# Pooled-key attention and channel mix on one core: the left-over keys of both heads of a pair in one matmul on a tile of 32 rows by 128 columns, in front of the burst

## The chip, the core and the metric

The kernel runs on one core of one Trainium2 chip. The metric is device time in microseconds (us), the median of several runs; lower is better.

## What is computed

Attention over pooled keys, then a channel mix (a gated feed-forward layer) on the attention's output. Batch 8, 8 heads, 576 tokens, head dimension 64; keys and values are averaged over groups of 8 tokens, so that 72 keys are left for each head.

```python
k_p = k.reshape(B, H, Sp, pool, D).mean(axis=3)
v_p = v.reshape(B, H, Sp, pool, D).mean(axis=3)
scores = scale * np.matmul(q, k_p.transpose(0, 1, 3, 2))
scores = scores - np.max(scores, axis=-1, keepdims=True)
attn = np.exp(scores)
attn = attn / (np.sum(attn, axis=-1, keepdims=True) + 1e-09)
attn_out = np.matmul(attn, v_p)              # the second product
# x: the heads side by side, 512 channels
xk = mu_k * x + (1.0 - mu_k) * x_prev        # x_prev: x one token earlier
xr = mu_r * x + (1.0 - mu_r) * x_prev
k = np.maximum(xk @ w_k, 0.0)
v = k * k @ w_v
r = 1.0 / (1.0 + np.exp(-(xr @ w_r)))
return r * v
```

## The kernel before, in words

The 4,608 tokens are cut into 13 chunks: one of 128, one of 256 and eleven of 384 tokens. For each chunk the scores, the softmax, the second product, the token shift and the three matrix products of the channel mix (`hidden`, line 1182, `gate`, line 1231, `mixed`, line 1264) are issued. A small list scheduler (class `Order`) decides at build time in which order the steps of all chunks stand on each engine; each step tells it the engine and a length, and it takes due times from a table (`EARLIER`). The order is fixed in the built program. TensorE does nearly all of the time's work: the channel mix alone runs as triples of matmuls on a high and a low part of each operand.

The change is in `quarters`, which makes the second product of one of the eleven chunks of 384 tokens (chunks 2 to 12). The 72 keys of a head are split into 64 main keys and 8 left-over keys. The probabilities come out of VectorE's transposes 32 rows by 32 columns at a time: `pth` (line 926) holds those of the main keys, `ptq` (line 955) those of the left-over keys. Each of the four 32-row groups of the array (index `t`) takes one quarter of the chunk's tokens, 96 columns, and writes its own PSUM bank of the four-bank tile `quad`. For each pair of heads `g` (4), three products `j` are added up: two blocks of 32 main keys (`j` 0 and 1, weights `vq_main`) and the left-over keys (`j` 2, weights `vq_rest`). In a 32-row group the left-over rows are 4 heads by 8 keys; `vq_rest` has a copy of the values for every head with zeros in the rows of the other heads, and so picks its head. For each of the two heads `m` of a pair the product goes to its own half of the array's columns. So a chunk has 4 x 3 x 4 x 2 = 96 matmuls, each on a tile of 32 rows by 64 columns, all at line 1033 and all on end: a burst. A matmul on fp32 data runs as two passes, each a weight load (PEld in the profile) and a matmul (PE), so that a burst has 192 of each.

What stands around a burst on TensorE are matmuls on the whole array of 128 by 128: those of `gate` or `hidden` in front of it, those of `mixed` or `gate` behind it. The scores of three tokens' tiles (line 795) form a similar burst, on tiles of 64 rows by 64 columns. Behind a burst ScalarE reads `quad` (`t`, line 1085), VectorE reads it (`xm`, line 1127), and ScalarE and GpSimd split the result into `xkh`, `xkl`, `xrh` and `xrl` for the next chunk. From chunk 7 on `hidden` places an alignment instruction (line 1174) on TensorE's queue, which fills up to 64 slots with NOPs, or branches over more, so that the next burst begins at a fixed place in a block of 256 instructions.

Of the kernel before, what the change touches and what calls it, by code (L numbers as in the profile page):

```python
# [17 lines left out]
B, H, S, D = 8, 8, 576, 64  # L18
# [4 lines left out]
NPAIR = H // 2  # L23
# [237 lines left out]
def attention_then_channel_mix(  # L261
# [13 lines left out]
    nc = tc.nc  # L275
# [28 lines left out]
    vq_main = [const.tile([P, 4, NPAIR, D], F32, name=f"vq_main{i}") for i in range(2)]  # L304
    vq_rest = [const.tile([P, 2, 4, D], F32, name=f"vq_rest{i}") for i in range(2)]
# [11 lines left out]
    def operand(kind, c):  # L317
        if c in WHOLE:
            return whole_operands[kind]
        if (kind, c) not in operands:  # L320
            whole = {"pth": range(len(CHUNKS)), "xkh": WHOLE_HID, "xrh": WHOLE_GATE, "sh": WHOLE_MIX, "ptq": range(len(CHUNKS))}.get(kind, ())
            dtype = F32 if c in whole else F32R
            operands[kind, c] = sb.tile(shapes[kind], dtype, name=f"{kind}_{c}", tag=kind)
        return operands[kind, c]
# [40 lines left out]
    for tag, n in EARLY:  # L365
        t = sb.tile([P, n, 2 * POOL * KEYS], F32, name=f"early_{tag}", tag=tag)
# [638 lines left out]
    def ready(c):  # L1005
        mine = [i for i, t in enumerate(tiles) if t[0] == c]
        return (
            *[(k, i) for i in mine for k in ("main", "side")], "om",
            *([("rest", 0)] if c in WHOLE_ATT else [("late rest", b) for b, *_ in units[c]]),
            *[("values", b, p) for b, *_ in units[c] for p in range(2)], *([] if c in WHOLE_ATT else [("turned", b) for b, *_ in units[c]]),  # L1010
        )

    def quarters(c):

        yield need(*ready(c))
        sc = yield take("sc")
        hi = yield take("hi")
        yield "pe", 2.75, False
        main = operand("pth", c).rearrange("p g n -> p (g n)").rearrange("p (i j k) -> p i j k", j=16, k=32)
        rest = operand("ptq", c)  # L1020
        quad = joint["quad"]
        out = quad[:, :, :CH].rearrange("p t (g i k) -> p t g i k", g=NPAIR, k=32)
        batch = [next(b for b, _, n, at in units[c] if at <= CH // 4 * t < at + n) % 2 for t in range(4)]
        for g in range(NPAIR):
            for j in range(3):
                for t, i in enumerate(batch):
                    rows = slice(32 * t, 32 * t + 32)
                    for m in range(2):
                        if j < 2:
                            w, p = vq_main[i][rows, (t - 2 * m - j) % 4, g], main[rows, :, 4 * g + 2 * m + j, :]  # L1030
                        else:
                            w, p = vq_rest[i][rows, g // 2, 2 * (g % 2) + m], rest[rows, :, g // 2, :]
                        nc.tensor.matmul(  # L1033
                            out=out[m * D:(m + 1) * D, t, g], lhsT=w, rhs=p, start=(j == 0), stop=(j == 2),
                        )
        for g in range(NPAIR):
            held["out", c, g] = quad[:, :, g * CH // 4:(g + 1) * CH // 4]
            order.make(("attended", c, g))
        held["quad", c] = [sc, hi, NPAIR]
# [274 lines left out]
    for c, n in enumerate(CHUNKS):  # L1314
        if c not in WHOLE_ATT:
            order.add(att_due[c], quarters(c), SPARE)
        for g in range(NPAIR):
            order.add(att_due[c] + g, attended(c, g), SPARE if c > 1 else 0.0)
            if c in WHOLE:
                order.add(att_due[c] + g + 6, later_joined(c, g))  # L1320
        for jt in range(NJT):
            order.add(begin[c] + 0.0455 * n * jt / NJT, hidden(c, jt), 1.0 if c else 0.0)
        for tt in range(n // P):
            order.add(begin[c] + 0.0455 * n + 2.8 * tt, gate(c, tt))
            order.add(begin[c] + (0.0455 + 0.022) * n + 5.5 * tt, mixed(c, tt))
# [56 lines left out]
```

## Time and profile before

| what | value |
|---|---|
| runs (3) | 597.18, 598.83 and 599.61 us; median 598.83 |
| profiled execution, span from first to last instruction | 595.8 us |
| median of the runs less that span | 3.0 us |
| TensorE matmuls busy | 588.2 us, 99% of the span |
| weight loads busy | 508.3 us, 85% |
| VectorE, ScalarE, GpSimd busy | 58%, 49%, 38% |
| line 1033's share of the chain that ended last | 4% |
| granted TensorE clock | 1.000 (2.4 GHz), mean over the span |

The page gives the profiled execution's span alone; its own time is not listed apart from the three runs. The chain that ended last is followed back from the last instruction; from 146.6 us on it consists of TensorE's pieces alone, up to the last 4 us.

### The profile page before, as it was taken

To read this page: it belongs to the slowest core of one execution; us is meant where nothing else is said; L and a number is where in the kernel's file an instruction comes from. 1 tells how busy PE (TensorE), PEld (TensorE's weight loads), DVE (VectorE), ACT (ScalarE), POOL (GpSimd) and SP (SyncE) were. 2 spreads that over 40 slices of the span, in tenths; PEclk is the share of its full clock that TensorE was granted. 3 is DMA by queue.
4 is the path that set the end of the run, shared out by engine and by line. 5 is a ranking of instruction groups with operands and counts; after the bars stand their busy time and mean duration, and the time that the engine had idled before them with its cause. 6 is when DMAs were issued, how large, how long until landed. Compare 5 with 4: busy or idle time off the path is not lost.

```text
span 595.8 us, 14121 instructions
## 1 busy us (share of the span) xinstructions
PE 588.2 (99%) x5822; PEld 508.3 (85%) x5822; DVE 348.5 (58%) x709; ACT 294.3 (49%) x574; POOL 224.9 (38%) x350
## 2 busy tenths in 40 slices
PE   9999999999999999999999999999999999999997
PEld 8986458888989989988988988988988988988985
DVE  4989956876438725944814944664824833834411
ACT  4777665844462453553642552462652643554420
POOL 2520269458051552346232257148114115115000
PEclk9999999999999999999999999999999999999999
DMA  8697422442005214113003221521201101000001
GB/s 308 212 390 287 157 77 89 137 157 72 2 19 204 73 46 165 73 57 96 20 12 120 95 73 57 192 73 56 78 2 62 47 1 40 15 3 36 19 0 53
DMA packets 23055, 54.72 MB, mean 92 GB/s; under 512 B 2896, under 2 KB 6352, under 8 KB 22992
## 3 DMA queue, kind: packets, MB, share of 16 engines
q1 hardware_dynamic: 22992, 53.82, 25.8%
q8 instruction: 46, 0.75, 0.5%
q14 instruction: 17, 0.14, 0.1%
HBM read 41.23 MB, written 9.44 MB: 85 GB/s over the span
## 4 chain that ended last, share of the span: by engine, by line
PE 84%; DVE 5%; POOL 4%; DMA 3%; ACT 2%; issue 1%; SPq 1%; DVEq 0%; POOLq 0%; ACTq 0%
PE mm L1264 26%; PE mm L1182 24%; PE mm L1231 11%; PE bank L1182 6%; PE quad L1033 4%; PE bank L1231 4%; PE bank L1264 4%; PE quad L795 3%; DMA got_wr<-in_w_r 2%; POOL stage L577 1%; POOL xkl L1153 1%; POOL xrl L1153 1%; PE own L441 1%; DVE xm L1127 1%; DVE stage L577 1%
## 5 line engine op out<-in xcount | busy, mean ns | idle before, releaser
L1182 PE MATMUL mm<-xkh,w_k 128*128 128x384 f32 x576 | 147.5, 336 | 1.2 <-DVE rk L1199 0.9
L1264 PE MATMUL mm<-w_v,sh 128*128 128x512 f32 x464 | 146.8, 392 | 0.0
L1127 DVE SCALAR_TENSOR_TENSOR xm<-quad,given,t 128x384 f32<-128x384 f32 x88 | 50.3, 613 | 109.2 <-ACT t L1085 72.5
L1182 PEld LDWEIGHTS mm<-xkh,w_k 128*128 128x128 f32 x576 | 103.6, 188 | 3.2 <-DVE rk L1199 1.7
L1264 PEld LDWEIGHTS mm<-w_v,sh 128*128 128x128 f32 x464 | 87.1, 188 | 19.0
L1182 PE MATMUL mm<-xkl,w_k 128*128 128x384 f32 x288 | 96.5, 335 | 0.5 <-POOL xkl L1153 0.5
L1264 PE MATMUL mm<-w_v,sl 128*128 128x512 f32 x232 | 90.4, 390 | 0.0
L1205 ACT CAST sh<-rk 128x384 fp32r<-128x384 f32 x88 | 45.1, 512 | 58.8 <-DVE rk L1199 58.6
L881 POOL TENSOR_TENSOR px<-e,sm 128x64 f32<-128x64 f32 (+1 forms) x33 | 13.7, 414 | 157.3 <-DVE sm L871 79.9
L1231 PE MATMUL mm<-w_r,xrh 128*128 128x512 f32 x192 | 61.3, 391 | 0.0
L1207 DVE TENSOR_TENSOR sl<-rk,sh 128x384 fp32r<-128x384 f32 x88 | 53.4, 608 | 12.8 <-ACT sh L1205 12.7
L1274 DVE TENSOR_TENSOR rs<-mm,rs 128x512 f32<-128x512 f32 x32 | 22.0, 688 | 64.9 <-PE mm L1264 64.5
L1153 POOL TENSOR_TENSOR xkl<-xm,xkh 128x384 fp32r<-128x384 f32 x44 | 44.3, 1019 | 41.3 <-ACT xkh L1151 41.3
L1182 PEld LDWEIGHTS mm<-xkl,w_k 128*128 128x128 f32 x288 | 54.1, 188 | 1.1 <-POOL xkl L1153 1.1
L1192 ACT ACTIVATE rk<-mm 128x384 f32<-128x384 f32 x72 | 35.0, 487 | 39.4 <-PE mm L1182 38.4
L1085 ACT ACTIVATE t<-quad,om_sb 128x384 f32<-128x384 f32 x88 | 44.9, 580 | 17.7 <-PE quad L1033 17.7
L1264 PEld LDWEIGHTS mm<-w_v,sl 128*128 128x128 f32 x232 | 43.6, 188 | 8.8
L577 POOL TENSOR_TENSOR stage<-stage 128x512 f32<-128x512 f32 (+4 forms) x56 | 48.1, 862 | 7.5 <-DMA stage<-in_vm 4.9
L1153 POOL TENSOR_TENSOR xrl<-xm,xrh 128x384 fp32r<-128x384 f32 x44 | 44.3, 1017 | 3.0 <-ACT xrh L1151 3.0
L1199 DVE SCALAR_TENSOR_TENSOR rk<-mm,rk 128x384 f32<-128x384 f32 x72 | 39.6, 550 | 8.3 <-ACT rk L1192 7.2
L1231 PEld LDWEIGHTS mm<-w_r,xrh 128*128 128x128 f32 x192 | 36.0, 188 | 7.7
L1231 PE MATMUL mm<-w_r,xrl 128*128 128x512 f32 x96 | 37.5, 390 | 0.0
(159 smaller groups left out, 978.6 us busy)
## 6 DMA issues: line engine op xcount, KB each, us to landing
qs<-in_qT SPq DMA_DIRECT2D x36, 256.0 KB, 4.1
out<-rs SPq DMA_DIRECT2D x36, 256.0 KB, 2.0
stage<-in_kT SPq DMA_DIRECT2D x15, 576.0 KB, 5.4
stage<-in_vm SPq DMA_DIRECT2D x15, 512.0 KB, 6.2
got_wk<-in_w_k SPq DMA_DIRECT2D x8, 512.0 KB, 6.8
got_wv<-in_w_v SPq DMA_DIRECT2D x8, 512.0 KB, 10.4
stage<-in_vr SPq DMA_DIRECT2D x6, 512.0 KB, 3.5
got_wr<-in_w_r SPq DMA_DIRECT2D x4, 512.0 KB, 8.6
```

The lines of the kernel that those rows point to most:

```text
L577: nc_eng.tensor_tensor(out=st[:, :, :w], in0=st[:, :, :w], in1=st[:, :, w:2 * w], op=ALU.add)
L1033: nc.tensor.matmul(out=out[m * D:(m + 1) * D, t, g], lhsT=w, rhs=p, start=(j == 0), stop=(j == 2),)
L1085: nc.scalar.activation(out=by_token(ts[m][:, 1:n + 1]), in_=xp, func=AF.Copy, scale=om_sb[:, m, g:g + 1])
L1127: nc.vector.scalar_tensor_tensor(out=by_token(xm[:, :n]), in0=bank[:, :n] if c in WHOLE_ATT else bank, scalar=mu_sb[:, m, g:g + 1], in1=by ...
L1153: nc.gpsimd.tensor_tensor(out=lo, in0=xm[:, :n], in1=hi, op=ALU.subtract)
L1182: nc.tensor.matmul(out=hp, lhsT=w[:, o], rhs=x[:, ct, :n], start=(ct == 0 and k == 0), stop=(ct == NCT - 1 and k == len(terms) - 1),)
L1192: nc.scalar.activation(out=rk[:, :n], in_=hp, func=AF.Relu)
L1199: nc.vector.scalar_tensor_tensor(out=rk[:, :n], in0=hp, scalar=0.0, in1=rk[:, :n], op0=ALU.max, op1=ALU.mult)
L1205: nc.scalar.copy(out=sh[:, :n], in_=rk[:, :n])
L1207: nc.vector.tensor_tensor(out=operand("sl", c)[:, jt, :n], in0=rk[:, :n], in1=sh[:, :n], op=ALU.subtract)
L1231: nc.tensor.matmul(out=bank, lhsT=x[:, ct, o], rhs=w, start=(ct == 0 and k == 0), stop=(ct == NCT - 1 and k == len(terms) - 1),)
L1264: nc.tensor.matmul(out=bank, lhsT=s[:, o], rhs=w, start=(jt == 0 and k == 0), stop=(jt == NJT - 1 and k == len(terms) - 1),)
```

## The change

The left-over keys are taken out of the inner loop. They come first, for all four pairs, and the two heads of a pair share one matmul: its weights are two neighbouring blocks of `vq_rest`, 128 columns, its output all 128 partitions, its tile 32 rows by 128 columns. The first of them in each bank opens the sums of the whole bank, and the last of the 64 main matmuls closes them. A burst has 16 + 64 = 80 matmuls, or 160 passes.

```diff
         for g in range(NPAIR):
-            for j in range(3):
+            for t, i in enumerate(batch):
+                rows = slice(32 * t, 32 * t + 32)
+                nc.tensor.matmul(
+                    out=out[:, t, g],
+                    lhsT=vq_rest[i][rows, g // 2, 2 * (g % 2):2 * (g % 2) + 2].rearrange("p m d -> p (m d)"),
+                    rhs=rest[rows, :, g // 2, :], start=(g == 0), stop=False,
+                )
+        for g in range(NPAIR):
+            for j in range(2):
                 for t, i in enumerate(batch):
                     rows = slice(32 * t, 32 * t + 32)
                     for m in range(2):
-                        if j < 2:
-                            w, p = vq_main[i][rows, (t - 2 * m - j) % 4, g], main[rows, :, 4 * g + 2 * m + j, :]
-                        else:
-                            w, p = vq_rest[i][rows, g // 2, 2 * (g % 2) + m], rest[rows, :, g // 2, :]
                         nc.tensor.matmul(
-                            out=out[m * D:(m + 1) * D, t, g], lhsT=w, rhs=p, start=(j == 0), stop=(j == 2),
+                            out=out[m * D:(m + 1) * D, t, g], lhsT=vq_main[i][rows, (t - 2 * m - j) % 4, g],
+                            rhs=main[rows, :, 4 * g + 2 * m + j, :], start=False, stop=(j == 1 and g == NPAIR - 1),
                         )
```

How the instructions of TensorE stand around the burst of chunk 3, before (the columns are line, operation, output and operands, and the output's shape; a row is one or more matmuls, each of them two passes):

```order
L1264 MATMUL mm0_115<-w_v7_1173,sh_2_989 128x512
L1033 MATMUL quad_724<-pth_3_1038,vq_main1_72 64x96 x16
L1033 MATMUL quad_724<-ptq_3_1028,vq_rest1_74 64x96 x8
L1033 MATMUL quad_724<-pth_3_1038,vq_main1_72 64x96 x16
L1033 MATMUL quad_724<-ptq_3_1028,vq_rest1_74 64x96 x8
L1033 MATMUL quad_724<-pth_3_1038,vq_main1_72 64x96 x16
L1033 MATMUL quad_724<-ptq_3_1028,vq_rest1_74 64x96 x8
L1033 MATMUL quad_724<-pth_3_1038,vq_main1_72 64x96 x16
L1033 MATMUL quad_724<-ptq_3_1028,vq_rest1_74 64x96 x8
L1264 MATMUL mm2_117<-w_v0_973,sh_2_989 128x512
```

And with the change:

```order
L1269 MATMUL mm0_115<-w_v7_1157,sl_2_999 128x512
L1269 MATMUL mm0_115<-w_v7_1157,sh_2_973 128x512
L1027 MATMUL quad_724<-ptq_3_1012,vq_rest1_74 128x96 x16
L1037 MATMUL quad_724<-pth_3_1022,vq_main1_72 64x96 x64
L1269 MATMUL mm2_117<-w_v0_957,sh_2_973 128x512
```

The neighbours are the same; the four groups of 8 left-over matmuls have become one group of 16 of double width, and the burst changes its tile shape once, inside.

On VectorE, the transposes that feed the burst of chunk 7 stand as before, the last one of `ptq` ahead of the last one of `pth`:

```order
L1199 SCALAR_TENSOR_TENSOR rk_86<-mm_116,rk_86 128x384
L955 STREAM_TRANSPOSE ptq_3094<-px_91 128x64
L1207 TENSOR_TENSOR sl_3059<-rk_86,sh_3030 128x384
L926 STREAM_TRANSPOSE pth_3108<-pm_90 128x512
L1127 SCALAR_TENSOR_TENSOR xm_83<-quad,given,t_80 128x384
```

This order is the same in the changed program (its line numbers are 5 higher behind the change), and so are those of ScalarE, GpSimd and SyncE.

## Rows read from the trace of the kernel before

**Rows 1.** The page: TensorE's busy time, and the granted clock in 40 slices.

```profile
PE 588.2 (99%) x5822; PEld 508.3 (85%) x5822; DVE 348.5 (58%) x709; ACT 294.3 (49%) x574; POOL 224.9 (38%) x350
...
PEclk9999999999999999999999999999999999999999
```

**Rows 2.** The chain that ended last, 250 to 310 us: start, length, piece.

```profile
251.17 5.44 PE mm L1231 x24
256.61 2.54 PE quad L1033 x143
259.15 5.67 PE mm L1264 x24
```

**Rows 3.** The same chain, 70 to 150 us, the first burst and what follows.

```profile
75.20 2.56 PE quad L1033 x151
...
91.09 1.02 POOL xkl L1153
92.15 8.78 PE mm L1182 x49
```

**Rows 4.** Tile `quad`: count, shortest/median/longest ns, first and last start, shape.

```profile
L1033 PEld LDWEIGHTS quad<-pth,vq_main x1408: 127/131/133, 75.1 to 533.5; 32*64 32x64 f32 x176
L1033 PE MATMUL quad<-pth,vq_main x1408: 240/241/293, 75.1 to 533.6; 32*64 32x96 f32 x176
L795 PEld LDWEIGHTS quad<-kbd,qs x960: 129/133/134, 64.8 to 506.1; 64*64 64x64 f32 x192
L795 PE MATMUL quad<-kbd,qs x960: 222/223/275, 64.8 to 506.1; 64*64 64x72 f32 x192
L1033 PE MATMUL quad<-ptq,vq_rest x704: 240/241/291, 75.5 to 533.7; 32*64 32x96 f32 x176
```

**Rows 5.** Timeline, 256.0 to 259.8 us, PE: start, length, work, count.

```profile
256.22 0.39 PE L1231 MATMUL mm<-w_r,xrh 128*128 128x512 f32 x1
256.54 0.59 PE L1033 MATMUL quad<-pth,vq_main 32*64 32x96 f32 x32
...
258.76 0.39 PE L1033 MATMUL quad<-ptq,vq_rest 32*64 32x96 f32 x11
259.08 0.50 PE L1264 MATMUL mm<-w_v,sh 128*128 128x512 f32 x1
259.42 0.39 PE L1264 MATMUL mm<-w_v,sl 128*128 128x512 f32 x1
```

**Rows 6.** Timeline of the same stretch, PEld (weight loads).

```profile
256.54 0.40 PEld L1033 LDWEIGHTS quad<-pth,vq_main 32*64 32x64 f32 x32 [0.35 <-DVE kbd L619]
...
259.08 0.19 PEld L1264 LDWEIGHTS mm<-w_v,sh 128*128 128x128 f32 x1
259.19 0.19 PEld L1264 LDWEIGHTS mm<-w_v,sl 128*128 128x128 f32 x1
```

**Rows 7.** Windows, weight loads of tile `quad`: stretch, length, busy (running or begun in it).

```profile
256.53:256.93 0.40, 0.39 (x34) 1.00 0.00 0
256.92:256.94 0.02, 0.02 (x5) 1.00 0.00 0
256.94:257.35 0.41, 0.41 (x36) 1.00 0.00 0
```

**Rows 8.** Timeline, 229.4 to 232.6 us, PE: a burst of scores on four tiles.

```profile
229.83 1.73 PE L795 MATMUL quad<-kbd,qs 64*64 64x72 f32 x96
231.49 0.62 PE L1182 MATMUL bank<-xkh,w_k 128*128 128x384 f32 x2
```

**Rows 9.** Timeline, 389 to 394.2 us, VectorE, ahead of the burst at 393.97.

```profile
391.66 0.25 DVE L955 STREAM_TRANSPOSE ptq<-px 128x64 f32<-128x64 f32 x1 [0.19 <-POOL px L881]
392.66 0.71 DVE L926 STREAM_TRANSPOSE pth<-pm 128x512 f32<-128x512 f32 x1 [0.76 <-POOL pm L886]
```

**Rows 10.** Line 1174, the alignment: count, ns, first and last start.

```profile
L1174 PEldq NOP  x156: 13/13/13, 374.3 to 514.4; - x156
L1174 PEldq COMPARE_BRANCH  x1: 192/192/192, 328.4 to 328.4; - x1
```

## The prediction

> **What bounds the kernel now.** I read the page first: TensorE is busy for 99% of the span, at a granted clock of 1.0 (2.4 GHz) from the first slice to the last [rows 1]. Then the chain of waits: around a burst of the second product it is an unbroken row of TensorE's pieces, the burst's 2.54 us among them [rows 2]. Only early is it otherwise: behind the first burst the chain leaves TensorE and comes back through GpSimd's `xkl` [rows 3], but that work starts from the burst's result, so a longer burst delays it too. So what one burst gains or loses counts once, and there are (1,408 + 704) / 192 = 11 bursts [rows 4]. What other engines wait is of no matter unless TensorE waits for them. The third view is the timeline of one burst, and there three prices are to be seen.
>
> *The burst's length.* The first pass starts at 256.54. The last group of records starts at 258.76 and ends 0.39 later, at 259.15; a pass has 0.24 us on record, so the last one starts at 258.91 [rows 4, 5]. From first start to last start it is 2.37 us for 192 passes.
>
> *What limits it.* Passes on one tile follow one another, those on different tiles run side by side. The score burst shows the pace of a tile: 96 passes on four tiles are 24 on each; its records end at 229.83 + 1.73 = 231.56, so the last pass starts 0.22 earlier, 1.51 after the first [rows 4, 8]. Less 0.05 for the first weight load (below), 23 steps take 1.46 us: 0.063 for 72 columns, hence about 0.084 for 96 columns. Eight tiles with 24 passes each would need 24 x 0.084 = 2.0 us, not 2.37. The rest is supply: 34 weight loads, 17 matmuls, begin in the first 0.40 us, just before 256.94 only 5 are under way where eight tiles want work, and then the next 31 to 36 come in 0.41 us [rows 7]. So the burst is fed in groups of 34 passes per 0.41 us, 12 ns a pass, and its tiles are close behind (34 x 0.084 / 8 = 0.36).
>
> *Changing the tile shape.* Between the burst's last start, 258.91, and the first load for the whole array, 259.08, lie 0.17 us [rows 5, 6]. The last pass needs 0.08 of it, so 0.09 are empty: no load is drawn ahead over the change of shape. Then the load itself is exposed: the first whole-array matmul takes 0.50 in place of 0.39, and the second load begins 0.11 behind the first [rows 5, 6]. A load of 128 columns takes 0.11 us. A load of 64 columns takes 0.05, which is what the longest pass, a first one, has over the median (293 against 241, and 275 against 223) [rows 4]. That holds for 32 rows and for 64 alike.
>
> **The change part by part**, for one burst.
>
> *The left-over stretch.* Before, it was 64 of 192 passes, 0.79 us of the 2.37. Now 16 matmuls, 32 passes, run on four tiles, 8 on each. Streaming still takes 0.084 a pass. Each pass also needs 128 columns of weights, and no row shows such a load on 32 rows. Its bounds are 0.05 (a 32-row load of 64 columns) and 0.11 (a 128-row load of 128 columns). Since 32 and 64 rows cost the same, I take it by columns: 0.11. One load can be prepared behind a running pass, but 0.11 is longer than 0.084, so the load sets the step: 8 x 0.11 = 0.88 us from the first load to the last pass's start. With the low bound it is 0.11 + 7 x 0.084 = 0.70. The groups of 34 could supply these 32 passes in 0.39, so that fewer instructions gain nothing here.
>
> *The change of shape inside the burst.* It is new: 32 x 128 to 32 x 64. Bounds: nothing, if tiles of the same 32 rows may follow each other freely, or what the burst's end costs, 0.09 empty behind the 0.08 of streaming and the load exposed. The trace has only changes to and from the whole array; I take their price: 0.17 until the first main load starts. The Trainium skill (TensorEngine Tiling (Array Packing), Key Properties) says that changing the tiling mode, not just the tile, drains TensorE; that speaks against this change. By that rule the price is paid, as in the sum here; without it the time is that of the first rival. The whole-array edges of rows 5 and 6 agree with it.
>
> *The main stretch.* 128 passes of the old kind, starting as the old burst does with a full queue of waiting instructions and an exposed load of 0.05, take their share of the old time: 2.37 x 128 / 192 = 1.58 us.
>
> *Sum.* 0.88 + 0.17 + 1.58 = 2.63 against 2.37: 0.26 us longer, times 11 bursts 2.9 us. The edges to the whole array stay. The left-over operand is now read first, which adds no wait: in the nearest case `ptq` is complete at 391.91 and `pth` at 393.37, ahead of the burst at 393.97 [rows 9], and the order on VectorE is unchanged. ScalarE's reads started behind the whole burst and still do. A burst has 64 instructions less on TensorE's queue, so the alignment has to skip more slots than its limit of 64: 39 and 64 make 103, and branches take the place of the 39 NOPs per chunk. NOPs and a branch are on the sequencer [rows 10]; the 34 passes that wait in the queue [rows 7] last longer than the 0.19 us of a branch, so they cost nothing; if that cover were gone, four more branches of 0.19 cost 0.8 us. Nothing is queued behind a new wait, and no DMA is moved.
>
> The profiled execution's span becomes 595.8 + 2.9 = 598.7 us; the median of the runs lies 3.0 above the span, hence 601.7 us.
>
> **The rivals.**
>
> *No drain between the two shapes of 32 rows.* For it: the row groups stay the same, so each could go on by itself. Against it: only changes at which nothing is drawn ahead are on record. The 0.09 and the exposed 0.05 fall away: 0.26 - 0.14 = 0.12 a burst, 1.3 us in all, 600.1. Chance 0.17.
>
> *The wide load hides.* If a 32-row load of 128 columns takes no more than a pass, the stretch is 0.70: 0.08 a burst, 0.9 us, 599.7. For it: a quarter of the array's weights. Against it: 32 and 64 rows cost the same [rows 4]. Chance 0.13. With both rivals together it would be 0.06 less than before, -0.7 us.
>
> *Faster: the supply decides.* If a burst is only as long as its instructions take to arrive, 32 passes less at 12 ns are worth 0.39 us, 4.2 us in all: 594.6. For it: the groups of rows 7, at which tiles stand idle. Its place is the left-over stretch, and it decides only if four tiles take 8 passes each in 0.39 us, 0.05 a pass; against it stands the tile's pace of 0.084 in rows 8, where nothing is short of supply. Chance 0.12.
>
> *Much slower: load and pass one after the other.* If the load on a row group waits for the pass on it, a step is 0.11 + 0.084, the stretch 1.55: 0.93 a burst, 10.2 us, 609.0. Against it: the pace of 0.063 for 72 columns in rows 8 leaves no room for a load of 0.05 between passes on the same rows. The Trainium skill (TensorE: Matmul & The Clock Gate, Part 3, The mechanism) has that rule: weight loads overlap passes in flight only where the row group differs. By that rule the time is this rival's; rows 8 disagree with it. Chance 0.06.
>
> That the change doesn't do what it says is left no chance: the order shows 16 wide matmuls ahead of 64. Other causes: 0.02.
>
> **How the numbers follow.** The forecast has 0.50, and 601.7 is its time. The highest bound of its costs, 0.10 for the drain and 0.112 for a load, makes 0.30 a burst, 3.3 us. I leave out the much slower rival and the faster one, 0.18 with 0.02 for other causes. What is left reaches from -0.7 to +3.3 us, and the three runs lie up to 1.7 from their median; half of that at each end, as a median of runs scatters less: 597.3 to 603.0. A measurement can tell about 0.5%, 3.0 us, from no change. The forecast lies just inside that and comes out beyond it somewhat less than half the time: 0.22, and with the much slower rival and a little of the others 0.30 for slower. Faster is the supply rival, 0.12. The rest, 0.58, is no change that can be told.
>
> **What would show it.** In the profile after, TensorE must have 11 x 32 = 352 passes fewer. A burst's last start should lie 2.6 us behind its first; the 32 wide loads should start over some 0.8 us, four at a time, 0.11 apart on a tile; the first main load 0.17 behind the last wide pass. If the first main passes start among the last wide ones, the first rival is right; if the wide steps are 0.084, the second; if the burst is about 2.0 us long, the third. The prediction is wrong altogether if TensorE has new waits outside the bursts, or if the bursts differ by less than 0.05 us from before and the time moves all the same.

## Result and profile after

The changed kernel takes 601.44 us (median of 4 runs, 600.76 to 602.81); the kernel before, measured beside it, 598.07 us. The ratio is 1.0056, with a 95% interval of 1.0038 to 1.0074: about 3.4 us slower, just beyond the 0.5% that a measurement can tell from no change. The forecast was 601.7 us.

The page of the changed kernel, as in [rows 1]:

```profile
span 599.1 us, 13265 instructions
...
PE 590.9 (99%) x5470; PEld 510.5 (85%) x5470; DVE 347.9 (58%) x709; ACT 294.3 (49%) x574; POOL 224.8 (38%) x350
...
PEclk9999999999999999999999999999999999999999
```

TensorE has 5822 - 5470 = 352 passes fewer and is busy 2.7 us longer. The granted clock is at its upper level (2.4 GHz) from the first slice to the last, and the busy times of VectorE, ScalarE and GpSimd have moved by 0.6 us at most. The span has grown by 599.1 - 595.8 = 3.3 us.

The chain that ended last, as in [rows 2] (start, length, piece), at the third burst, a middle one and the last:

```profile
157.40 1.08 PE quad L1027 x32
158.47 1.76 PE quad L1037 x99
...
257.81 1.08 PE quad L1027 x32
258.88 1.76 PE quad L1037 x98
260.64 5.67 PE mm L1269 x24
...
534.37 1.08 PE quad L1027 x32
535.44 1.76 PE quad L1037 x102
```

The same chain of the kernel before, at the third and the last burst:

```profile
156.79 2.54 PE quad L1033 x152
...
531.41 2.54 PE quad L1033 x147
```

A burst's piece was 2.54 us long, and the whole-array matmuls behind it start right after; now it is 1.08 + 1.76 = 2.84. That is 0.30 more. From the third burst's start to the last one's, 374.62 us have become 376.97: 2.35 more in 8 steps, 0.29 a burst, and behind the last burst's start it is 0.34 more. So from the third burst on nothing else has moved, and nine bursts account for 2.7 of the 3.3 us.

The other 0.61 was lost in front of the third burst. That two bursts of 0.30 stand there too is a coincidence in this pair of profiles. The first burst starts 0.32 early (74.88 against 75.20 [rows 3]), and `hidden` behind it 0.28 early (91.87 against 92.15): what that burst lost, the other engines' work behind it has won back. The second burst, at 123.6 us, is not on the chain at all, before or after. From 108 to 147 us the chain runs through transfers and the other engines. At 113 us the changed kernel is still 0.3 ahead; then it falls behind, at a transfer that VectorE waits for (the chain after):

```profile
113.61 2.36 DMA vq_main<-vq_main
...
116.33 0.76 DVE stage L577
```

and before:

```profile
115.71 0.76 DVE stage L577
```

That is 0.62 later, and 0.61 of it is left at the third burst. In the other profiles below, the third burst starts anywhere from 0.3 to 1.9 us later than before, and not by the length of the bursts: 0.33 later where they are as long as before, 1.59 later where they are shorter.

Inside a burst there are three pieces. First tile `quad`, as in [rows 4]:

```profile
L1037 PE MATMUL quad<-pth,vq_main x1408: 240/242/293, 75.9 to 537.0; 32*64 32x96 f32 x176
...
L1027 PE MATMUL quad<-ptq,vq_rest x352: 269/271/346, 74.8 to 535.2; 32*128 32x96 f32 x176
```

The timeline of one burst, PE, as in [rows 5]:

```profile
257.74 1.15 PE L1027 MATMUL quad<-ptq,vq_rest 32*128 32x96 f32 x32
258.81 1.83 PE L1037 MATMUL quad<-pth,vq_main 32*64 32x96 f32 x128
260.57 0.50 PE L1269 MATMUL mm<-w_v,sh 128*128 128x512 f32 x1
```

A group's last pass starts one record before its end. The last wide pass starts at 257.74 + 1.15 - 0.27 = 258.62, 0.88 behind the first. The first main pass starts at 258.81, 0.19 later. The last main pass starts at 258.81 + 1.83 - 0.24 = 260.40, 1.59 later, and 0.17 after that the whole array's first. From first to last start it is 2.66 us; it was 2.37 [rows 4, 5].

The pace of the wide loads, in windows of the weight loads on `quad` as in [rows 7]:

```profile
257.73:257.84 0.11, 0.10 (x4) 1.00 0.00 0
257.84:257.95 0.11, 0.11 (x8) 1.00 0.00 0
...
258.80:259.20 0.40, 0.39 (x34) 1.00 0.28 51
```

In the first 0.11 us four loads run, by the kernel's order one on each tile; in the next four run on and four begin. The main stretch opens as the old burst did, with 34 in 0.40 us.

Line 1179, the alignment, as in [rows 10]:

```profile
L1179 PEldq COMPARE_BRANCH  x5: 170/175/309, 330.2 to 514.6; - x5
```

There are five branches and no NOPs, as foreseen. The steps from the third burst on are an even 0.25 to 0.31 longer each, with a branch in them or not, so the branches cost nothing.

### The profile page after: what moved, and what is told of

Its sections match the earlier page's. It is cut to its first block, busy times and chain, and to the rows that moved or that the text cites. A ratio compares the mean times of both kernels' runs of the same rounds, so it can differ in the third digit from the quotient of the medians.

```text
span 599.1 us, 13265 instructions
## 1 busy us (share of the span) xinstructions
PE 590.9 (99%) x5470; PEld 510.5 (85%) x5470; DVE 347.9 (58%) x709; ACT 294.3 (49%) x574; POOL 224.8 (38%) x350
## 4 chain that ended last, share of the span: by engine, by line
PE 89%; POOL 4%; DVE 3%; DMA 2%; ACT 2%; issue 1%; SPq 0%; DVEq 0%; POOLq 0%; ACTq 0%
PE mm L1187 27%; PE mm L1269 26%; PE mm L1236 11%; PE bank L1187 6%; PE bank L1236 4%; PE bank L1269 4%; PE quad L1037 3%; PE quad L795 3%; PE quad L1027 2%; POOL stage L577 1%; PE bank L451 1%; POOL xkl L1158 1%; PE mm L588 1%; POOL xrl L1158 1%; DMA stage<-in_kT 1%
## 6 DMA issues: line engine op xcount, KB each, us to landing
qs<-in_qT SPq DMA_DIRECT2D x36, 256.0 KB, 4.1
out<-rs SPq DMA_DIRECT2D x36, 256.0 KB, 2.0
```

## The experiments

**Narrow ones in front.** The edit, against the changed kernel:

```diff
-                nc.tensor.matmul(
-                    out=out[:, t, g],
...
+                for m in range(2):
+                    nc.tensor.matmul(
+                        out=out[m * D:(m + 1) * D, t, g], lhsT=vq_rest[i][rows, g // 2, 2 * (g % 2) + m],
+                        rhs=rest[rows, :, g // 2, :], start=(g == 0), stop=False,
+                    )
```

> The left-over matmuls stand in front of the burst as in the change, but stay 32 of 32 x 64, so that no tile shape changes inside the burst. Theory (wide load plus change of shape): a burst is as before, 2.37 us from first to last pass start, and the time is that of the kernel before, within 0.5 us. Rival (the order costs: left-over operand read first, sums of a bank left open through the burst): a burst is 2.66 us as in the change, the time 3.3 us above before.

Measured: 598.06 us beside 598.02, ratio 1.0006 (0.9993 to 1.0019). Its chain:

```profile
256.93 0.91 PE quad L1028 x53
...
259.47 5.66 PE mm L1269 x24
```

From 256.93 to 259.47 it is 2.54 us, as before. That the left-over keys come first, and that the sums are opened and closed by other matmuls, costs nothing. So what each burst loses belongs to the double width: the wide loads and the change of shape that they bring.

**Wide ones behind.** The 16 wide matmuls stand after the 64 main ones; the main ones open the sums, the wide ones close them. The edit, against the kernel before:

```diff
         for g in range(NPAIR):
-            for j in range(3):
+            for j in range(2):
...
+                            rhs=main[rows, :, 4 * g + 2 * m + j, :], start=(g == 0 and j == 0), stop=False,
                         )
+        for g in range(NPAIR):
+            for t, i in enumerate(batch):
...
+                    rhs=rest[rows, :, g // 2, :], start=False, stop=(g == NPAIR - 1),
+                )
```

> The wide left-over matmuls stand behind the main ones. Theory: same wide steps of 0.112 us and one change of shape, so a burst of 2.6 to 2.7 us and 3.0 to 3.6 us above before. Rival (what costs is that the main matmuls no longer start with the burst and its full queue): the main stretch ends at 1.59 us as in the change, and the burst is shorter than 2.5 us, under 1.5 us above before.

Measured: 602.78 us, ratio 1.0081 (1.0059 to 1.0104). The chain and, below it, the PE timeline of the same kernel:

```profile
258.94 1.76 PE quad L1029 x104
260.70 1.08 PE quad L1036 x32
261.78 5.67 PE mm L1269 x24
```

```profile
260.63 1.15 PE L1036 MATMUL quad<-ptq,vq_rest 32*128 32x96 f32 x32
261.71 0.50 PE L1269 MATMUL mm<-w_v,sh 128*128 128x512 f32 x1
```

The pieces are the same, 1.76 and 1.08, in the other order; for the burst's length the place doesn't matter, and the rival is out. The last wide pass starts at 260.63 + 1.15 - 0.27 = 261.51, and the whole array follows 0.20 later, where behind a narrow pass it is 0.17. So the way out of a wide pass is 0.02 to 0.03 longer, as its record is (0.27 against 0.24), whether it leads to the tiles of 32 x 64 (0.19 above) or to the whole array. The total is 4.8 us above the kernel before it, where 3.0 to 3.6 were expected, and 1.3 above the changed kernel's. The first burst begins at 76.2 us in its profile and at 74.8 in that of the change, so this lies ahead of the edited work and isn't put down to it.

**A change of shape for each pair.** The second loop over pairs is dropped, so that each pair has its four wide matmuls and then its 16 main ones: seven changes of shape instead of one.

```diff
                 )
-        for g in range(NPAIR):
             for j in range(2):
```

> Each pair's four wide matmuls stand in front of that pair's main ones: the same 80 matmuls, but seven changes of shape inside a burst in place of one. Theory (each change costs the end of the streaming, a drain of about 0.09 us and an exposed load): a pair takes 0.22 + 0.18 + 0.30 + 0.17 = 0.87 us, a burst 3.3 us, the time 10 us above before. Rival (the change of shape costs nothing by itself, the wide loads are all of the loss): a burst of 2.66 us, 3.3 us above before.

Measured: 610.41 us, ratio 1.0209 (1.0188 to 1.0229).

```profile
260.82 0.41 PE quad L1027 x8
261.23 0.52 PE quad L1036 x32
...
264.51 5.66 PE mm L1268 x24
```

The burst is 264.51 - 260.82 = 3.69 us long against 2.84. Six more changes cost 0.85 us, 0.14 each. That is 0.2 more than expected. The PE timeline of the first pair shows where:

```profile
260.75 0.48 PE L1027 MATMUL quad<-ptq,vq_rest 32*128 32x96 f32 x8
261.16 0.59 PE L1036 MATMUL quad<-pth,vq_main 32*64 32x96 f32 x32
261.67 0.48 PE L1027 MATMUL quad<-ptq,vq_rest 32*128 32x96 f32 x8
```

The last wide pass starts at 260.75 + 0.48 - 0.27 = 260.96, and the first main pass 0.20 later; the last main pass starts at 261.16 + 0.59 - 0.24 = 261.51, and the next wide one 0.16 later. So the change of shape has its price in both directions, and near the 0.18 and 0.17 that the theory took. What it had too short are the 32 main passes between two changes: 0.35 us from first start to last, in place of 0.30, four times a burst.

**Each wide matmul in two.** Its 96 columns are cut into 64 and 32: the weights are loaded twice as often, the same columns streamed.

```diff
+                for k in (slice(0, 2), slice(2, 3)):
                     nc.tensor.matmul(
-                        out=out[:, t, g],
+                        out=out[:, t, g, k],
...
```

> Each wide matmul is made twice, on 64 and on 32 of its 96 columns, with the weights loaded for each: as many columns stream as in the change, by twice as many loads. Theory (the load of 128 columns sets the step): 16 steps of 0.112 us on a tile in place of 8, a burst of 3.56 us, 13 us above before. Rival (the step is the streaming, and a wide pass of 96 columns takes 0.112 us): the wide stretch stays under 1.0 us, the burst under 2.8 us, at most 5 us above before.

Measured: 609.78 us, ratio 1.0188 (1.0162 to 1.0214).

```profile
260.23 1.98 PE quad L1028 x64
262.20 1.76 PE quad L1038 x106
```

32 more passes without a column more to stream made the wide stretch 1.98 - 1.08 = 0.90 us longer, which on each of four tiles is 8 x 0.112. So a pass on this tile takes 0.112 us whether it streams 96 columns or 64 and 32. A rule that counts streamed columns, or load plus columns, is out. That it is the load that sets the step is read from its length: 0.11 is also what separates two loads of 128 columns for the whole array [rows 6]. The burst came out as expected (3.56 from first to last start, 1.98 + 1.76 - 0.17 = 3.57), the time at 11.5 us above before in place of 13.

**Left-over keys of one head only.** The kernel before, with 32 narrow passes fewer and no wide ones: it leaves out the left-over keys of one head of each pair.

```diff
-                    for m in range(2):
+                    for m in (g % 2,) if j == 2 else range(2):
...
```

> The kernel before without the left-over product of one head of each pair (the first head in two pairs, the second in the other two): that part of the result is missing. It has 80 narrow matmuls a burst, as many as the change, and no change of shape; a tile has 20 passes in place of 24. Supply theory (groups of 34 passes per 0.41 us): 2.37 x 160 / 192 = 1.97 us, 4.4 us below before. Tile pace alone: 0.05 + 20 x 0.083 = 1.71 us, 7.3 us below before. Either way it bounds what 16 matmuls less can be worth without a wide tile.

Measured: 597.83 us beside 598.31, ratio 0.9988 (0.9970 to 1.0007). Both theories missed it. The chain, and one of TensorE's waits (in total, times, longest):

```profile
158.38 2.31 PE quad L1033 x124
...
531.80 2.31 PE quad L1033 x124
```

```profile
PE mm L1264 <- issue: 0.3, 1, 0.3
```

A burst is only 0.23 shorter, in some 0.20. From the third to the last burst's start it is 373.42 us instead of 374.62, so 1.20 of 8 x 0.2 = 1.6 are kept there, the 0.3 at line 1264 taken off. The third burst itself starts 1.6 us late, in the stretch where other engines and transfers hold the chain and where the other profiles scatter too. A shorter burst thus pays in full from 157 us on; the early part lost as much in this profile. Whether the shorter bursts caused that wasn't tried.

**Only the first pair wide.** Four wide matmuls, 24 narrow left-over ones, 64 main ones: the drain is kept, three quarters of the wide loads go.

```diff
-        for g in range(NPAIR):
+        for g in range(1):
             for t, i in enumerate(batch):
...
+        for g in range(1, NPAIR):
+            for t, i in enumerate(batch):
+                rows = slice(32 * t, 32 * t + 32)
+                for m in range(2):
+                    nc.tensor.matmul(
+                        out=out[m * D:(m + 1) * D, t, g], lhsT=vq_rest[i][rows, g // 2, 2 * (g % 2) + m],
...
```

> Only the first pair's left-over keys are wide (4 matmuls, 2 steps on a tile), those of the other three pairs stay narrow: one change of shape, a quarter of the wide loads. Theory (0.18 us for the change, 0.026 us a pair for the wide loads): 0.40 us until the first narrow load, then 88 matmuls at the old pace, 2.17 us: a burst of 2.58 us, 2.3 us above before. Rival (the wide loads are all of it): a quarter of the loss, a burst of 2.44 us, 0.8 us above before.

Measured: 611.5 us, ratio 1.0209 (1.0167 to 1.0250), 13.5 us above before, where the theories had 2.3 and 0.8. The chain:

```profile
205.52 2.55 issue
...
262.98 0.41 PE quad L1027 x8
...
265.76 4.31 PE mm L1277 x18
...
311.61 1.34 issue
...
386.14 0.74 issue
```

An ordinary burst is 265.76 - 262.98 = 2.78 us long, 0.24 more than before, close to the theory. The rest are stalls that the other kernels don't have: 2.55 and 1.34 us inside two bursts, and 0.74 to 0.8 us ahead of four more. TensorE's clock in windows around the first and behind the second (length, busy time and count of each engine, clock, DMA share, GB/s):

```profile
198.00:203.00 5.00, 5.00 (x30) 4.79 (x28) 4.88 (x12) 1.81 (x4) 1.22 (x2) 1.00 0.29 92
205.28:208.06 2.78, 0.24 (x15) 0.07 (x4) 1.56 (x3) 1.72 (x3) 2.62 (x4) 0.92 0.16 62
208.06:214.00 5.94, 5.93 (x43) 4.64 (x43) 0.00 (x0) 0.27 (x1) 2.98 (x6) 0.50 0.01 4
...
311.40:313.00 1.60, 0.26 (x23) 0.07 (x7) 0.00 (x0) 0.00 (x0) 0.00 (x0) 1.00 0.00 0
313.00:319.00 6.00, 6.00 (x37) 4.92 (x37) 1.87 (x4) 4.49 (x9) 2.67 (x7) 1.00 0.01 3
```

Behind the 2.78 us with hardly a pass the granted clock is 0.50 of full, 1.2 GHz instead of 2.4, for 6 us: about another 3 us lost. Behind the shorter second stall it stayed at 1.00. Of the four runs one took only 607.83 us, with a mean granted clock of 1.000 where the others, 611.28 to 612.09, had 0.994 to 0.997: there the clock did not fall so far or so long.

The 0.74 lie behind the alignment (line 1187), which here just fits its limit and so fills up with NOPs, 55 for each of four chunks:

```profile
L1187 PEldq NOP  x220: 13/13/13, 382.9 to 527.9; - x110
```

The first 55 start from 382.9 to 386.8, and the next weight load at 386.85. That is 3.9 us for 55, or 0.07 each, though each is recorded as 13 ns, and longer than the work in the queue lasted. In three of the four places the view names VectorE's `ptq` for the wait, which had ended 0.2 to 0.3 us earlier; in the last of them too the NOPs go on to 527.9, and the load follows at 527.97.

**The same kernel, aligned.** To learn whether the mixture of shapes or the place of the instructions was to blame, only the two constants of the alignment were changed.

```diff
-ALIGNED_FROM = 7
+ALIGNED_FROM = 4
-MOST_PADS = 64
+MOST_PADS = 0
```

> The kernel with only the first pair wide (four wide and 24 narrow left-over matmuls), as before, but the alignment instruction stands from chunk 4 on instead of 7, and always branches (no NOPs). Theory: in the earlier run of that kernel the tile shapes cost 0.236 us a burst, 2.6 us in all, and the other 11 us came from where its instructions lay: two bursts across two borders of 256 instructions (stalls of 2.78 and 1.56 us and the slower clock behind one of them) and 55 NOPs in a row ahead of four others (0.9 us each). With the bursts at their places and no NOPs all of that goes: no piece of TensorE's with an issue stall over 0.3 us around a burst, bursts of 2.60 to 2.65 us, and a time of 600 to 602 us, ratio 1.003 to 1.006. Rival: the stalls belong to the mixture of shapes itself (four wide passes at a time between narrow ones) and come whatever the place: 608 to 612 us again, ratio over 1.016. Between: if only the NOPs' part goes, 607.8.

Measured: 601.64 us beside 598.26, ratio 1.0053 (1.0028 to 1.0078). Its chain, TensorE's waits and the alignment's line:

```profile
258.42 0.41 PE quad L1027 x8
...
261.20 5.67 PE mm L1277 x24
```

```profile
PE quad L1045 <- issue: 0.5, 1, 0.5
```

```profile
L1187 PEldq COMPARE_BRANCH  x8: 163/163/179, 191.9 to 514.9; - x8
```

Some 10 us are gone with nothing but the alignment changed. The burst is 2.78 us long, 0.24 more than before, as in the run above. One stall of 0.5 is left, at 206 us, which is more than the 0.3 expected; a branch of the alignment stands ahead of that burst too (191.9), so why it is left stays open. Eleven bursts at 0.24 would be 2.6 us, with that stall 3.1; measured were 3.4, with an interval of 1.7 to 4.7. So the three other pairs, made wide, add only a little (2.84 against 2.78), and most of the loss comes with the first wide pair: the change of shape.

## Why the prediction was right

**What bounds the kernel**: right for nine of the eleven bursts. From the third one on TensorE's chain is unbroken, and each burst adds its 0.29. For the first two it was not shown: the prediction let a longer burst delay the early chain too, but in these profiles the first burst's loss was won back behind it, and the second is off the chain. A 0.61 from elsewhere took their place, which was luck. Over several runs it stays open whether they count. The interval of the ratio, 2.3 to 4.4 us, holds nine and eleven bursts alike; of the two largest losses, 12.4 us with a change of shape for each pair is nearer eleven bursts (12.6) than nine (10.4), and 11.5 with each wide matmul in two is nearer nine (10.8) than eleven (13.2).

**The left-over stretch**: 0.88 predicted, 0.88 measured. Of the two bounds for a load of 32 rows by 128 columns, 0.05 and 0.11, the upper one held. It goes by columns and not by rows (0.112 here, 0.11 on 128 rows), and it hides the streaming, as the run that cut the matmuls in two shows. This fells the rivals "the wide load hides" and "load and pass one after the other". The rule of the Trainium skill behind the latter (TensorE: Matmul & The Clock Gate, Part 3, The mechanism) is not borne out: four tiles with 8 passes each on the same rows took 0.112 a step, the load's time alone.

**The change of shape**: 0.17 predicted, 0.19 measured; with it the rival "no drain" fell. The 0.02 or 0.03 are what this term lacked: it took the price from an edge behind a narrow pass, and the second experiment shows the way out of a wide pass to be 0.03 longer. That makes a burst 0.29 longer instead of 0.26, which is what the upper bound given comes to (0.26 with 0.01 for the drain and 0.02 for the loads; the prediction wrote 0.30). The Trainium skill (TensorEngine Tiling (Array Packing), Key Properties) has the drain for a change of tiling mode; the 0.14 for each further change agrees with it.

**The main stretch**: 1.58 predicted, 1.59 measured. The rule behind it, 12 ns for each pass, did not hold with one head left out, where 160 passes should have taken 1.97 us and took 2.31 - 0.17 = 2.14; so that the supply of passes sets these 1.59 is not shown.

**The sum**: 3.3 us in place of 2.9. The time came out 0.3 us below the forecast and not above it, because the second addend was too large: the median of before itself went from 598.83 us in three runs to 598.07 in four, 2.3 us above its profiled span and not 3.0. Each run takes 1.8 us more than its own span (600.92 against 599.1 in the profile after); the other 1.2 of the 3.0 is that the profiled execution was a quick one, among runs that lie up to 2.4 apart. Two misses of 0.4 to 0.7 us offset each other; the burst's length is the better proof. The prediction gave its largest chance, 0.58, to a change too small to tell; the measured 0.56%, with an interval of 0.38% to 0.74%, lies on that border.

**What was costed at nothing**: the order of the products (first experiment) and the branches (even steps of the bursts) cost nothing. That a row of NOPs isn't free once it is longer than the queue was seen only in the run with 55.

**The faster rival**: rightly thought unlikely, but its price was wrong. It took 12 ns a pass from the groups of 34 in [rows 7], so 0.39 us for 32 passes. Removed outright, 32 passes were worth 0.20 to 0.23. A reading that was not tested: the groups of 34 are themselves paced, the next one coming only as passes of the last one end, and then a rate read off them is not what the supply would do by itself.

## What to carry to other kernels

Merging two matmuls into one of double width saves passes, not time, when the weight load is then longer than the streaming it hides behind: compare load time per column with the columns streamed before counting instructions. Price each change of tile shape inside a run of small matmuls (0.14 to 0.19 us here), and group the shapes so that there is one. Whenever an edit changes how many instructions stand between two bursts, look for "issue" stalls in the profile and re-place the alignment before judging the edit: the kernel with one wide pair took 611.5 or 601.64 us by that alone. And before multiplying a burst's loss by the number of bursts, follow the chain through each of them.

## What the runs showed of the hardware that was not expected

*Instructions can run out inside a burst.* In the kernel with one wide pair the trace has transfers of 16 KB in the instruction queue that start at 205.78 and 310.52 us; the stalled bursts go on at 208.07 and 312.94. In the aligned one a transfer starts at 203.85 and the stall ends at 206.17. That is 2.3 to 2.4 us from the start of a transfer to the first pass that waited for it, each time. The first stall's window (DMA view of the kernel with one wide pair):

```profile
q8 instruction: 1, 0.02, 2.0%
```

Such a burst has 92 x 4 = 368 instructions in 2.6 us, so it goes through a block of 256 in 1.8 us, less than those 2.3 to 2.4. That the stalls belong to the instructions' place is shown by the aligned run; that a border between blocks inside the burst is the cause is read from these transfers, and not tried by itself. The Trainium skill (Runtime: NRT & Kernel Launch, Instruction fetch mechanics) has blocks of 256 instructions and calls crossing a border mostly hidden; here it was hidden in 9 of 11 bursts and cost 1.34 and 2.55 us in the others.

*The clock after a stall.* In one profile the granted clock fell from 2.4 to 1.2 GHz in a stretch of 2.78 us with TensorE nearly idle (0.92 of full on its mean), and it stayed there for about 6 us of dense work behind it; around 1.6 us of the same kind it did not fall.
